# Weight preparation a step earlier, evictions ahead of maxima, and compact loads in the start-up of an attention and MLP kernel

## The chip, the cores and the metric

The kernel runs on one core of a Trainium2 chip. The metric is device time in microseconds (us) of one execution; the time of a kernel is the median of several runs. TensorE does the matrix products, VectorE, ScalarE and GpSimd everything between them, SyncE issues nearly all transfers. The profile calls them PE (its weight loads PEld), DVE, ACT, POOL and SP.

## The reference

Windowed attention, then a token mix of low rank, then an MLP over channels, all with residuals:

```
B, H, S, D = 8, 8, 576, 64
s = (q @ k^T) / sqrt(D)                     # per batch and head
keep, heads 0..3: 0 <= i-j < 32
keep, heads 4..7: 0 <= i-j < 128 and (i-j) % 4 == 0
a = softmax over kept;  x = (a @ v) as (B, S, H*D)       # 8 x 576 x 512
u = x + (U @ V)^T mixed over tokens:  h = x^T @ U @ V,  u = x + h^T   # U 576x32, V 32x576
out = u + relu(u @ w1) @ w2                 # w1 512x2048, w2 2048x512
```

The weights U, V, w1 and w2 arrive as 64-bit floats and are used as a high and a low part of 32 bits.

## The kernel before, in words

The 4608 tokens are 36 tiles of 128; three tiles make a chunk of 384 tokens, so there are 12 chunks. In each chunk the MLP runs over 16 blocks f of 128 hidden channels. Block f is `layer1(f)`, twelve products into the PSUM tile `ph` (high weight by high input, low by high, high by low, four each), then two evictions: ACT writes the high half `hh` with the relu (L912) and DVE the rest `hl` (L913). `layer2(f-1)` follows, nine products into `acc`. While a chunk runs, the attention and the token mix of later batches are put into slots between these products: `slot()` takes items from one queue that is sorted by due time.

Batch 0's attention runs ahead of chunk 0, in `first_batch`. Its unit is a group g, 64 query rows of two tiles by four heads; a batch has 9 groups. A group goes: scores `s` on PE (L404), `soften`, which is mask and maximum `nmax` on DVE (L423) and the exponential on ACT (L427), a transposition `ptp` on PE (L438), a copy to `pt` (ACT L686 here, DVE L444 later), `product`, the product `pv` with v (L461), and `place`, which divides by the sums (L467, L468) and writes the result to the x tiles or to `xp` (L491). For batch 0 `pv` has one PSUM buffer. Heads 4 to 7 are computed with the tokens in another order, so their results go from `xp` to the x tiles by DMA: for batch 0 through the DRAM tensor `spare` (`leave` L766, `come` L771), for later batches by the moves of L495 in `place`.

Batch 1's groups 9 to 17 run in the slots of chunk 0, along with batch 0's and 1's token mix (`t`, `m`, the split `xhl` of L510, `utl`). For batch 0, q and k come compact (tag `k`, 320 KB a group), and `spread_q` puts q into a zeroed tile of two diagonal blocks with two POOL copies (L320). For batch 1 they come as full blocks with the zeros (`qkr`, 224 KB for two heads, 18 loads, L350). v comes in two loads a group (L332), into three buffers; the second is behind `place`'s moves in SP's queue.

The 32 weight pieces, w1 and w2 of every f (piece NSMALL + 2f and the next; NSMALL is 3, the pieces of U and V), are prepared once, during chunk 0: `send` issues the DMA of the raw 64-bit words (L188, L190, 512 KB a piece, five buffers `raw` until the last two blocks), `narrowed` takes two passes on ACT (L197, L198), `add_low` a shift (L202) and an add (L204) on DVE or POOL, and `finish` casts the high half (`w1h` on ACT L208, `w2h` on DVE L210) and subtracts it on POOL for the low (`w1l`, `w2l`, L211). `weight_step` does one of each for four successive pieces: finish of i−3, add of i−2, narrowing of i−1, and sends up to i + AHEAD. It is called twice a block. The instruction order on the engines is the order in which this program is written.

Of the kernel before, what the change touches and what calls it, by code (L numbers as in the profile page):

```python
# [10 lines left out]
F32 = mybir.dt.float32  # L11
# [14 lines left out]
P = 128  # L26
# [34 lines left out]
XL_DVE = ((1, 0),)  # L61
AHEAD = 2
POST_AT = 0.7
# [79 lines left out]
@with_exitstack  # L143
def attention_moe_kernel(ctx: ExitStack, tc: tile.TileContext, qk0, qk1, qk2, vv, masks, wide, ident, ut, vt, uv, w1, w2, out):
    nc = tc.nc
# [130 lines left out]
    def weight_step():  # L276
        i = at.get(0, NSMALL + 3)
        at[0] = i + 1
        if NSMALL <= i - 3 < NPIECE and i - 3 not in finished:
            if i - 3 == NSMALL + 2 * F_LAST:  # L280
                prep_open.close()
                make_w(F_LAST, FC, "right")
            finish(i - 3)
        if NSMALL <= i - 2 < NPIECE and i - 2 not in added:
            add_low(i - 2, nc.gpsimd if (i - NSMALL) % 2 else nc.vector)
        if NSMALL <= i - 1 < NPIECE and i - 1 not in scaled:
            narrowed(i - 1)
        send(min(NPIECE, i + AHEAD))

# [22 lines left out]
    def load_q(g):  # L312
        t = early.tile([P, UNITS, QB + KB], F32, tag="k", name=f"k{g}", bufs=NGB)
        nc.sync.dma_start(out=t, in_=qk0[g])
        loaded[g, 0] = t

    def spread_q(g):
        for i in range(2):
            rs = slice(i * QB, (i + 1) * QB)
            nc.gpsimd.tensor_copy(out=q_sb[rs, g % NQ, :, i], in_=loaded[g, 0][rs, :, 0:QB])  # L320

    def load_v(g, i):
        if (g, 1, i) in loaded:
            return
        if g < NGB:
            t = early.tile([KB, 2, UNITS, VW], F32, tag="v0", name=f"v{g}", bufs=NGB)
            nc.sync.dma_start(out=t, in_=vv[g])
            loaded[g, 1, 0] = t[:, 0]
            loaded[g, 1, 1] = t[:, 1]
        else:  # L330
            t = work.tile([KB, UNITS, VW], F32, tag="v", name=f"v{g}_{i}", bufs=3)
            nc.sync.dma_start(out=t, in_=vv[g][:, i])  # L332
            loaded[g, 1, i] = t

    N0 = UNITS * NGB
    N2 = N0 * SPLIT
    raws = {}
# [5 lines left out]

    def fetch(n, eng=nc.sync):
        if n >= UNITS * NG or n in raws:
            return
        if n < N2:
            if n % 2 == 0:
                raw = work.tile([P, 2, QK1], F32, tag="qks", name=f"qkr{n}", bufs=TB)
                eng.dma_start(out=raw, in_=qk1[n // UNITS - NGB][:, n % UNITS:n % UNITS + 2])  # L350
                raws[n] = raw[:, 0]
                raws[n + 1] = raw[:, 1]
        else:
            raw = work.tile([P, QK2], F32, tag="qk", name=f"qkr{n}", bufs=QKB)
            m = QK1 if is_odd(n) else QK2
            nc.sync.dma_start(out=raw[:, 0:m], in_=qk2[n - N2][:, 0:m])
            raws[n] = raw

# [20 lines left out]
    def score(g, u):  # L379
# [12 lines left out]
        else:  # L392
# [11 lines left out]
            nc.tensor.matmul(sp[:, u % sp.shape[1], :], lhsT=ql, rhs=kr, start=True, stop=True)  # L404
# [233 lines left out]
    def attention_steps(b):  # L638
# [3 lines left out]
        for s in range(NGB + LAG):  # L642
            g = NGB * b + s

            def pre(s=s, g=g):
                if b > 0 and 0 < s <= NGB:
                    load_v(g - 1, 0)
                if s >= LAG:
                    weighted(g - LAG, held.pop(g - LAG))
                if b > 0 and 0 < s <= NGB:  # L650
                    load_v(g - 1, 1)

# [6 lines left out]
            def some(us, g=g):  # L659
                for u in us:  # L660
                    score(g, u)
                for u in us:
                    n = UNITS * g + u
                    if n >= N2:
                        split_qk(n + LOOK)
                        fetch(n + LOOK + DMA_LOOK)
                    elif n >= N0 and n % 2 and n + 2 * TB - 1 < N2:
                        fetch(n + 2 * TB - 1)
                for u in us:
# [10 lines left out]
    def first_batch():  # L680
# [8 lines left out]
        for g in range(NGB):  # L689
# [18 lines left out]
            if g >= 1:  # L708
                copy(g - 1)
            if g >= 3:  # L710
                place(g - 3, pv.pop(g - 3))
            if g == 5:
                narrowed(0)
                add_low(0, nc.gpsimd)
                finish(0)
        w0, w1 = NSMALL, NSMALL + 1
        pv[7] = product(7, pt.pop(7))
        t_first(0, 0)
        turn_dilated(2)
        place(6, pv.pop(6))  # L720
        t_evict(0, 1)
# [108 lines left out]
    load_v(NGB - 1, 0)  # L830
    send(NSMALL + 4)
    for i in (0, 2):
        fetch(N0 + i)
    send(NSMALL + 5)
    fetch(N0 + 4)
    first_batch()
    psum_open.close()
    psum = ctx.enter_context(tc.tile_pool(name="psum", bufs=3, space=bass.MemoryType.PSUM))
# [49 lines left out]
    for c in range(NCHUNK):  # L888
# [41 lines left out]
        for f in range(FC):  # L930
            if c == 0 and f == 0:
                weight_step()
            if c == 0 and f == F_MID - 1:
                after_first()
            layer1(f)
            if f < FC - 1:
# [6 lines left out]
            if f > 0:  # L943
                layer2(f - 1)
                if f < FC - 1:
                    slot()
            if c == 0:
                weight_step()
        for t in more[2:]:
# [11 lines left out]
def lay_out(q, k, v, U, V, w1, w2):  # L961
# [6 lines left out]
    for half in range(2):  # L968
# [13 lines left out]
        for i in range(NJ // 2):  # L982
            g = TILES.index((half, 2 * i)) // 2
            for r in (slice(0, D), slice(D, P)):
                qk2[:, g, :, r, :P] = qp[SPLIT:, :, P * i:P * (i + 1)].transpose(0, 1, 3, 2)
                qk2[:, g, :, r, P:] = kp[SPLIT:, :, P * i:P * i + KW].transpose(0, 1, 3, 2)
    q0 = np.stack([q1[0, :, :, i, :, i] for i in range(2)], axis=2).reshape(NGB, UNITS, P, QB)
    qk0 = np.concatenate([q0, k1[0].reshape(NGB, UNITS, P, KB)], axis=-1)
    qk0 = np.ascontiguousarray(qk0.transpose(0, 2, 1, 3))
    qk1 = np.concatenate([q1.reshape(B, NGB, UNITS, P, P), k1.reshape(B, NGB, UNITS, P, KB)], axis=-1)  # L990
    qk2[:, ODD, :, :, :QK1] = qk1[SPLIT:, ODD]
    qk2 = qk2.reshape((B - SPLIT) * NGB * UNITS, P, QK2)
    qk1 = np.ascontiguousarray(qk1[1:SPLIT].reshape((SPLIT - 1) * NGB, UNITS, P, QK1).transpose(0, 2, 1, 3))
    vv = np.ascontiguousarray(vv.reshape(B * NGB, 2, KB, UNITS, VW).transpose(0, 2, 1, 3, 4))
# [17 lines left out]
    for p in range(NDP):  # L1012
# [35 lines left out]
```

## Time and profile before

| | |
|---|---|
| median of 3 runs | 1067.45 us (1066.99 to 1067.75) |
| the profiled execution | 1066.73 us |
| its span | 1064.6 us |
| PE busy, share of the span | 1000.8 us, 94% |
| DVE, ACT, POOL busy | 583.9, 381.8, 321.3 us |
| mean granted clock of PE | 0.976 |
| batch 0 | 0 to 49.5 us of the span |
| chunk 0 | 49.5 to about 212 us |

A profile line of a group names line, engine, operation and tiles, then how often it ran, its busy time, the mean of one in ns, and the idle time of its engine just before, with what ended it. A line of the waits reads: engine, its line, `<-` the one waited for, then us in total, times, and the longest. A line of the timeline or of the chain begins with start and length in us. The stretches of a window table give, for each part of the span, the busy time of the engines, the clock that PE was granted as a share of full speed, the busy share of the DMA engines, and GB/s.

### The profile page before, as it was taken

The numbers are of one execution on the slowest core, as the hardware profiler recorded it, in microseconds if no ns is written. First come the engines' busy times: TensorE is split into PE (matmuls) and PEld (weight loads), VectorE is DVE, ScalarE is ACT, GpSimd is POOL, SyncE is SP. The second block draws the span as 40 slices with busy tenths as digits, with TensorE's granted clock in tenths as the row PEclk, the third lists the DMA queues.
The fourth block names the chain that finished last, engine by engine and source line by source line (L and its number), as shares of the span: only waits on it lengthen the run. The fifth ranks groups of instructions, "written<-read, shape, count | busy, mean of one in ns | idle before, by whom it ended". The sixth has DMA issues, their size and how long they took to land.

```text
span 1064.6 us, 18031 instructions
## 1 busy us (share of the span) xinstructions
PE 1000.8 (94%) x5928; PEld 875.0 (82%) x5928; DVE 583.9 (55%) x1965; ACT 381.8 (36%) x937; POOL 321.3 (30%) x537
## 2 busy tenths in 40 slices
PE   6768877699999999999999999999999999999998
PEld 5556655588889888988888888988888888999897
DVE  3355565577645676476655675576746774411211
ACT  4453444544423343244514353244414352111110
POOL 3243344543503262133503252134404251000000
PEclk9987898899999999999999999999999999999999
DMA  9156742334322342344323342343323330400000
GB/s 271 68 167 183 218 147 79 110 115 120 100 73 74 89 128 72 76 128 112 87 70 92 102 123 57 89 122 110 89 79 97 91 110 15 129 1 1 30 1 30
DMA packets 97164, 102.54 MB, mean 96 GB/s; under 512 B 12624, under 2 KB 83792, under 8 KB 97072
## 3 DMA queue, kind: packets, MB, share of 16 engines
q1 hardware_dynamic: 97072, 101.39, 33.0%
q8 instruction: 48, 0.79, 0.3%
q14 instruction: 44, 0.36, 0.1%
HBM read 79.32 MB, written 17.89 MB: 91 GB/s over the span
## 4 chain that ended last, share of the span: by engine, by line
PE 86%; issue 4%; DVE 3%; DMA 2%; POOL 2%; SPq 1%; ACT 1%; DVEq 0%; POOLq 0%; ACTq 0%
PE ph L907 38%; PE acc L924 36%; PE pv L461 4%; PE s L391 3%; PE s L404 2%; PE t L540 2%; POOL w1l L211 1%; DVE v L204 1%; PE m L564 1%; DMA raw<-w 1%; SPq L495 1%; PE ptp L438 1%; DMA spare<-xp 1%; ACT hh L912 1%; DMA k<-qk 0%
## 5 line engine op out<-in xcount | busy, mean ns | idle before, releaser
L913 DVE SCALAR_TENSOR_TENSOR hl<-ph,hh 128x384 fp32r<-128x384 f32 x192 | 106.3, 554 | 233.0 <-ACT hh L912 232.1
L924 PE MATMUL acc<-w2h,hh 128*128 128x512 f32 x576 | 230.8, 401 | 0.0
L924 PE MATMUL acc<-w2l,hh 128*128 128x512 f32 x576 | 229.6, 399 | 0.0
L924 PE MATMUL acc<-w2h,hl 128*128 128x512 f32 x576 | 213.7, 398 | 0.0
L368 POOL TENSOR_TENSOR qks<-qkr,qks 128x160 fp32r<-128x160 f32 x192 | 102.8, 535 | 352.6 <-ACT qks L367 255.4
L907 PE MATMUL ph<-uth,w1h 128*128 128x384 f32 x768 | 172.5, 343 | 32.0 <-ACT w1h L208 30.5
L912 ACT ACTIVATE hh<-ph 128x384 fp32r<-128x384 f32 x192 | 93.5, 487 | 298.1 <-PE ph L907 286.9
L907 PE MATMUL ph<-uth,w1l 128*128 128x384 f32 x768 | 178.2, 350 | 5.6 <-POOL w1l L211 5.6
L907 PE MATMUL ph<-utl,w1h 128*128 128x384 f32 x768 | 181.1, 350 | 0.0
L907 PEld LDWEIGHTS ph<-uth,w1h 128*128 128x128 f32 x768 | 137.6, 190 | 51.9 <-ACT w1h L208 35.8
L427 ACT ACTIVATE p<-p,nmax 128x160 f32<-128x160 f32 (+1 forms) x288 | 109.3, 406 | 160.9 <-DVE nmax L423 159.8
L907 PEld LDWEIGHTS ph<-uth,w1l 128*128 128x128 f32 x768 | 140.0, 195 | 10.3 <-POOL w1l L211 10.0
L907 PEld LDWEIGHTS ph<-utl,w1h 128*128 128x128 f32 x768 | 141.5, 197 | 1.7 <-issue 0.2
L450 DVE STREAM_TRANSPOSE pt<-p 32x128 f32<-32x128 f32 x432 | 130.2, 301 | 17.8 <-ACT p L427 12.4
L924 PEld LDWEIGHTS acc<-w2h,hl 128*128 128x128 f32 x576 | 108.7, 189 | 23.7
L924 PEld LDWEIGHTS acc<-w2h,hh 128*128 128x128 f32 x576 | 109.6, 190 | 16.3 <-issue 0.4
L924 PEld LDWEIGHTS acc<-w2l,hh 128*128 128x128 f32 x576 | 109.2, 190 | 16.1
L367 ACT CAST qks<-qkr 128x288 fp32r<-128x288 f32 x192 | 81.1, 429 | 100.0 <-PE s L391 56.2
L420 DVE TENSOR_TENSOR p<-s,wide_sb 128x160 f32<-128x160 f32 x192 | 60.1, 320 | 72.1 <-PE s L391 69.7
L371 POOL TENSOR_TENSOR qks<-qkr,qks 64x128 fp32r<-64x128 f32 x192 | 90.5, 471 | 15.1
L510 POOL TENSOR_TENSOR xhl<-x,xhl 128x256 fp32r<-128x256 f32 (+1 forms) x65 | 47.7, 743 | 82.6 <-ACT xhl L508 75.2
L461 PEld LDWEIGHTS pv<-v,pt 96*64 96x64 f32 x1152 | 42.1, 142 | 30.1 <-issue 17.1
(82 smaller groups left out, 891.1 us busy)
## 6 DMA issues: line engine op xcount, KB each, us to landing
qkr<-qk SPq DMA_DIRECT2D x192, 144.0 KB, 2.2
raw<-w SPq DMA_DIRECT2D x26, 512.0 KB, 5.1
v<-vv SPq DMA_DIRECT2D x126, 97.5 KB, 2.1
out<-x SPq DMA_DIRECT2D x36, 256.0 KB, 2.2
zd<-z SPq DMA_DIRECT2D x120, 64.0 KB, 2.1
xt<-zd SPq DMA_DIRECT2D x30, 256.0 KB, 2.8
qkr<-qk SPq DMA_DIRECT2D x18, 224.0 KB, 2.7
raw<-w SPq DMA_DIRECT2D x12, 256.0 KB, 2.9
```

The lines of the kernel that those rows point to most:

```text
L367: nc.scalar.copy(out=t[:, 0:QK2], in_=raw)
L368: nc.gpsimd.tensor_tensor(out=t[:, QK2:], in0=raw[:, P:], in1=t[:, P:QK2].bitcast(F32), op=ALU.subtract)
L371: eng.tensor_tensor(out=t[lo, 0:P], in0=raw[lo, 0:P], in1=t[lo, 0:P].bitcast(F32), op=ALU.subtract)
L420: nc.vector.tensor_tensor(out=p_sb[:, u, :], in0=sp[:, 0:KW], in1=held[0][:, kind], op=ALU.add)
L427: nc.scalar.activation(out=p_sb[:, u, 0:w], in_=p_sb[:, u, 0:w], func=AF.Exp, bias=nmax[:, u:u + 1], scale=-1.0,)
L450: nc.vector.transpose(out=pt[WIN * k:WIN * (k + 1), :, rs], in_=p_sb[rs, :, o:o + WIN])
L461: nc.tensor.matmul(pv[rs, u, :], lhsT=pt[:, u, rs], rhs=loaded[g, 1, i][:, u, :], start=True, stop=True)
L510: eng.tensor_tensor(out=xl[rs], in0=x[rs], in1=xh[rs].bitcast(F32), op=ALU.subtract)
L907: nc.tensor.matmul(ph, lhsT=w[:, k, :], rhs=u[:, k, :], start=(n == 0), stop=(n == len(seq) - 1))
L912: nc.scalar.activation(out=hh, in_=ph, func=AF.Relu)
L913: nc.vector.scalar_tensor_tensor(out=hl, in0=ph, scalar=0.0, in1=hh.bitcast(F32), op0=ALU.max, op1=ALU.subtract)
L924: nc.tensor.matmul(acc[i], lhsT=h[:, ss], rhs=w, start=(f == 0 and n == 0), stop=(f == FC - 1 and n == 2))
```

## The change

Three edits, made together.

First, `place(g-3)` stands ahead of `product(g-2)` and of `soften(g)` in `first_batch`, and `place(6)` ahead of `product(7)`.

Second, batch 1's q and k come compact like batch 0's, in 9 loads of 320 KB, two groups ahead, and `spread_q` copies q into two zeroed tiles `q1` (four more memsets on DVE). Both v loads of a group are issued ahead of `weighted`, which holds `place` and its moves, and have four buffers; this order holds for all later batches too.

Third, `weight_step` starts one piece further on, and the step that closed a block now opens the next. All that a step does thus happens one step earlier relative to layer 1, and raws are sent up to i + 3 (i + 2 near the end). To start that way `first_batch` sends one piece more and narrows one piece more.

```
-AHEAD = 2
+AHEAD = 3
...
+    q1_sb = [work.tile([P, UNITS, 2, QB], F32, tag="z", name=f"q1_{i}", bufs=ZS) for i in range(2)]
...
     def weight_step():
-        i = at.get(0, NSMALL + 3)
+        i = at.get(0, NSMALL + 4)
...
-        send(min(NPIECE, i + AHEAD))
+        half = NSMALL + 2 * F_LAST
+        send(min(NPIECE, i + AHEAD if i + AHEAD <= half else max(half, i + 2)))
...
+    def q_of(g):
+        return q_sb[:, g % NQ] if g < NGB else q1_sb[g % 2]
+
     def spread_q(g):
         for i in range(2):
             rs = slice(i * QB, (i + 1) * QB)
-            nc.gpsimd.tensor_copy(out=q_sb[rs, g % NQ, :, i], in_=loaded[g, 0][rs, :, 0:QB])
+            nc.gpsimd.tensor_copy(out=q_of(g)[rs, :, i], in_=loaded[g, 0][rs, :, 0:QB])
...
-            t = work.tile([KB, UNITS, VW], F32, tag="v", name=f"v{g}_{i}", bufs=3)
+            t = work.tile([KB, UNITS, VW], F32, tag="v", name=f"v{g}_{i}", bufs=4)
...
             def pre(s=s, g=g):
-                if b > 0 and 0 < s <= NGB:
+                if 0 < s <= NGB:
                     load_v(g - 1, 0)
+                    load_v(g - 1, 1)
+                if b < SPLIT and s + 2 < NGB:
+                    load_q(g + 2)
+                if b < SPLIT and s + 1 < NGB:
+                    spread_q(g + 1)
                 if s >= LAG:
                     weighted(g - LAG, held.pop(g - LAG))
-                if b > 0 and 0 < s <= NGB:
-                    load_v(g - 1, 1)
...
     def first_batch():
...
+            if g >= 3:
+                place(g - 3, pv.pop(g - 3))
             if g >= 2:
                 pv[g - 2] = product(g - 2, pt.pop(g - 2))
...
-            if g >= 3:
-                place(g - 3, pv.pop(g - 3))
...
+        place(6, pv.pop(6))
         pv[7] = product(7, pt.pop(7))
...
-        place(6, pv.pop(6))
...
+        send(NSMALL + 6)
...
+        narrowed(w1 + 1)
...
-    send(NSMALL + 4)
-    for i in (0, 2):
-        fetch(N0 + i)
-    send(NSMALL + 5)
-    fetch(N0 + 4)
+    for i in range(3, 6):
+        send(NSMALL + i)
+        if i < 5:
+            load_q(NGB + i - 3)
     first_batch()
+    spread_q(NGB)
...
         for f in range(FC):
-            if c == 0 and f == 0:
-                weight_step()
             if c == 0 and f == F_MID - 1:
                 after_first()
+            if c == 0:
+                weight_step()
             layer1(f)
...
-            if c == 0:
-                weight_step()
```

ACT around the eviction of block 6, before. `v` and `raw` are the narrowing of a later piece, `p` the exponentials of a group, and the last row is the cast of block 7's w1:

```order
L912 ACTIVATE hh_6_1210<-ph_6_1197 128x384
L197 ACTIVATE v_1218<-raw_1131 128x512
L198 ACTIVATE raw_1131<-raw_1131 128x512
L427 ACTIVATE p_1247<-p_1247,nmax_1248 128x96 x4
L208 CAST w1h_1046<-v_1192 128x4x128
```

And after, the same place:

```order
L919 ACTIVATE hh_6_1227<-ph_6_1214 128x384
L209 CAST w1h_1054<-v_1145 128x4x128
L198 ACTIVATE v_1235<-raw_1065 128x512
L199 ACTIVATE raw_1065<-raw_1065 128x512
L428 ACTIVATE p_1266<-p_1266,nmax_1267 128x96 x4
```

The cast of w1 for block 7 has moved from behind the narrowing and the group's exponentials to right behind the eviction of block 6.

DVE at the same place, before: eviction `hl`, cast of w2, shift and add of block 7's w1 (v_1192), then `place` of a group.

```order
L202 TENSOR_SCALAR v_1128<-v_1128 128x512
L913 SCALAR_TENSOR_TENSOR hl_6_1211<-ph_6_1197,hh_6_1210 128x384
L210 CAST w2h_1048<-v_1128 128x512
L202 TENSOR_SCALAR v_1192<-v_1192 128x512
L204 ISA v_1192<-raw_1036,v_1192 128x1024
L467 TENSOR_SCALAR ssum_1240<-pv_1231 128x4
```

After; block 7's w1 is v_1145:

```order
L211 CAST w2h_1056<-v_1062 128x512
L203 TENSOR_SCALAR v_1145<-v_1145 128x512
L205 ISA v_1145<-raw_943,v_1145 128x1024
L920 SCALAR_TENSOR_TENSOR hl_6_1228<-ph_6_1214,hh_6_1227 128x384
L203 TENSOR_SCALAR v_1209<-v_1209 128x512
L468 TENSOR_SCALAR ssum_1261<-pv_1252 128x4
```

The cast of w2 and the shift and add of w1 have moved ahead of the eviction `hl`; behind it stands one shift of a later piece.

SP in block 3, before: a group's first v, the moves of `place`, the second v, then q and k:

```order
L188 DMA raw_704<-w 128x4x256
L190 DMA raw_733<-w 128x1024
L332 DMA v_0_740<-vv 96x260
L495 DMA x_425<-xp_754 16x256
L495 DMA x_757<-xp_754 32x256
L495 DMA x_759<-xp_754 16x256 x2
L495 DMA x_762<-xp_754 32x256
L495 DMA x_764<-xp_754 16x256
L332 DMA v_1_766<-vv 96x260
L350 DMA qkr_775<-qk 128x448
L350 DMA qkr_777<-qk 128x448
```

After:

```order
L189 DMA raw_721<-w 128x4x256
L191 DMA raw_750<-w 128x1024
L340 DMA v_0_757<-vv 96x260
L340 DMA v_1_759<-vv 96x260
L319 DMA k_761<-qk 128x640
L496 DMA x_408<-xp_777 16x256
L496 DMA x_780<-xp_777 32x256
L496 DMA x_782<-xp_777 16x256 x2
L496 DMA x_785<-xp_777 32x256
L496 DMA x_787<-xp_777 16x256
```

Both v loads and the load of q and k now stand ahead of the moves, one load in place of two.

More of the change, by code (lines that the diff above doesn't have):

```diff
@@ L143, in attention_moe_kernel @@
 @with_exitstack
-def attention_moe_kernel(ctx: ExitStack, tc: tile.TileContext, qk0, qk1, qk2, vv, masks, wide, ident, ut, vt, uv, w1, w2, out):
+def attention_moe_kernel(ctx: ExitStack, tc: tile.TileContext, qk0, qk2, vv, masks, wide, ident, ut, vt, uv, w1, w2, out):
     nc = tc.nc
@@ L312, in load_q @@
     def load_q(g):
-        t = early.tile([P, UNITS, QB + KB], F32, tag="k", name=f"k{g}", bufs=NGB)
+        if g < NGB:
+            t = early.tile([P, UNITS, QB + KB], F32, tag="k", name=f"k{g}", bufs=NGB)
+        else:
+            t = work.tile([P, UNITS, QB + KB], F32, tag="qks", name=f"k{g}", bufs=TB)
         nc.sync.dma_start(out=t, in_=qk0[g])
         loaded[g, 0] = t
+    def q_of(g):
+        return q_sb[:, g % NQ] if g < NGB else q1_sb[g % 2]
     def spread_q(g):
@@ L330, in load_v @@
         else:
-            t = work.tile([KB, UNITS, VW], F32, tag="v", name=f"v{g}_{i}", bufs=3)
+            t = work.tile([KB, UNITS, VW], F32, tag="v", name=f"v{g}_{i}", bufs=4)
             nc.sync.dma_start(out=t, in_=vv[g][:, i])
             loaded[g, 1, i] = t
-    N0 = UNITS * NGB
-    N2 = N0 * SPLIT
+    N2 = UNITS * NGB * SPLIT
     raws = {}
@@ L342, in is_odd, with fetch @@
         return n // UNITS % NGB == ODD
-    def fetch(n, eng=nc.sync):
+    def fetch(n):
         if n >= UNITS * NG or n in raws:
             return
[L347 to L357, printed above, removed]
+        assert n >= N2
+        raw = work.tile([P, QK2], F32, tag="qk", name=f"qkr{n}", bufs=QKB)
+        m = QK1 if is_odd(n) else QK2
+        nc.sync.dma_start(out=raw[:, 0:m], in_=qk2[n - N2][:, 0:m])
+        raws[n] = raw
     def split_qk(n):
@@ L398, in score @@
                 sp = state[g][2]
-            if g >= NGB:
+            if n >= N2:
                 fetch(n)
@@ L402, in score @@
             else:
-                ql, kr = q_sb[:, g % NQ, u].rearrange("p i q -> p (i q)"), loaded[g, 0][:, u, QB:]
+                ql, kr = q_of(g)[:, u].rearrange("p i q -> p (i q)"), loaded[g, 0][:, u, QB:]
             nc.tensor.matmul(sp[:, u % sp.shape[1], :], lhsT=ql, rhs=kr, start=True, stop=True)
@@ L666, in some @@
                         fetch(n + LOOK + DMA_LOOK)
-                    elif n >= N0 and n % 2 and n + 2 * TB - 1 < N2:
-                        fetch(n + 2 * TB - 1)
                 for u in us:
@@ L812, in attention_moe_kernel @@
         eng.memset(q_sb[i * QB:(i + 1) * QB, :, :, 1 - i], 0.0)
+    for i in range(2):
+        for q1 in q1_sb:
+            nc.vector.memset(q1[i * QB:(i + 1) * QB, :, 1 - i], 0.0)
     for t in ts0:
@@ L986, in lay_out @@
                 qk2[:, g, :, r, P:] = kp[SPLIT:, :, P * i:P * i + KW].transpose(0, 1, 3, 2)
-    q0 = np.stack([q1[0, :, :, i, :, i] for i in range(2)], axis=2).reshape(NGB, UNITS, P, QB)
-    qk0 = np.concatenate([q0, k1[0].reshape(NGB, UNITS, P, KB)], axis=-1)
+    q0 = np.stack([q1[:SPLIT, :, :, i, :, i] for i in range(2)], axis=3).reshape(SPLIT * NGB, UNITS, P, QB)
+    qk0 = np.concatenate([q0, k1[:SPLIT].reshape(SPLIT * NGB, UNITS, P, KB)], axis=-1)
     qk0 = np.ascontiguousarray(qk0.transpose(0, 2, 1, 3))
@@ L992, in lay_out @@
     qk2 = qk2.reshape((B - SPLIT) * NGB * UNITS, P, QK2)
-    qk1 = np.ascontiguousarray(qk1[1:SPLIT].reshape((SPLIT - 1) * NGB, UNITS, P, QK1).transpose(0, 2, 1, 3))
     vv = np.ascontiguousarray(vv.reshape(B * NGB, 2, KB, UNITS, VW).transpose(0, 2, 1, 3, 4))
@@ L1020, in lay_out @@
         "qk0": qk0,
-        "qk1": qk1,
         "qk2": qk2,
```

## The prediction

> **What bounds the kernel now.** I read the stretches of the span first, then what TensorE waited for, then the rows of one f-block. The columns of the stretches are: length, busy time with instructions of PE, PEld, DVE, ACT and POOL, the granted clock, the DMA share and GB/s.
>
> ```profile
> 49.50:105.00 55.50, 41.71 (x218) 35.46 (x220) 28.15 (x88) 25.96 (x60) 24.09 (x22) 0.78 0.52 160
> 105.00:156.00 51.00, 38.97 (x242) 31.30 (x242) 27.46 (x81) 20.75 (x49) 20.15 (x18) 0.87 0.59 186
> 156.00:212.00 56.00, 39.07 (x171) 31.56 (x168) 30.68 (x61) 25.75 (x62) 28.70 (x29) 0.88 0.33 100
> 212.00:1064.60 852.60, 847.71 (x5000) 750.39 (x4998) 477.99 (x1624) 286.41 (x707) 233.13 (x437) 1.00 0.29 82
> ```
>
> From 212 us on PE is idle for 852.6 − 847.7 = 4.9 us, and the change touches nothing there but the order of v loads. Everything to be won lies ahead of it: batch 0 (to 49.5 us) and chunk 0 (49.5 to 212 us), where PE idles for 162.5 − 119.75 = 42.75 us and the clock is reduced. Clock lost under PE's own work: 0.22 × 41.71 + 0.13 × 38.97 + 0.12 × 39.07 = 19.0 us. At full clock chunk 0 would hold 119.75 − 19.0 = 100.7 us of PE work, 6.3 us for each of 16 blocks. The waits of PE in 49 to 212 us, then of 173 to 212 us (blocks 12 to 15):
>
> ```profile
> PE ph L907 <- ACT w1h L208: 30.5, 14, 3.9
> PE ph L907 <- POOL w1l L211: 5.6, 13, 1.1
> ...
> PE ph L907 <- ACT w1h L208: 11.1, 4, 3.1
> PE ph L907 <- POOL w1l L211: 2.1, 4, 1.1
> ```
>
> So 36.1 of the 42.75 us are layer 1 waiting for its own weights. The eviction hh closes a block's layer 1; in the chain those of blocks 1 and 9 are 93.2 us apart, 11.7 us a block:
>
> ```profile
> 62.51 0.50 ACT hh L912
> ...
> 155.75 0.50 ACT hh L912
> ```
>
> Why the weights are late shows in block 6 (timeline):
>
> ```profile
> 121.49 0.49 ACT L912 ACTIVATE hh<-ph 128x384 fp32r<-128x384 f32 x1 [3.17 <-PE ph L907]
> 122.98 1.38 POOL L211 TENSOR_TENSOR w2l<-v,w2h 128x512 fp32r<-128x512 f32 x1 [3.17 <-DVE w2h L210]
> 123.28 1.64 DVE L204 CUSTOM_DVE_ANT_0 v<-raw,v 128x1024 uint16<-128x1024 uint16 x1
> 125.24 0.86 DVE L491 TENSOR_TENSOR x<-pv,ssum 64x256 f32<-64x256 f32 x2
> 126.49 1.17 ACT L427 ACTIVATE p<-p,nmax 128x96 f32<-128x96 f32 x4 [3.38 <-DVE nmax L423]
> 127.56 0.60 ACT L208 CAST w1h<-v 128x512 fp32r<-128x512 f32 x1
> 128.22 1.03 PE L907 MATMUL ph<-uth,w1h 128*128 128x384 f32 x4 [2.17 <-ACT w1h L208]
> 128.24 1.29 POOL L211 TENSOR_TENSOR w1l<-v,w1h 128x512 fp32r<-128x512 f32 x1 [3.88 <-ACT w1h L208]
> 129.59 1.65 PE L907 MATMUL ph<-uth,w1l 128*128 128x384 f32 x4 [0.34 <-POOL w1l L211]
> ```
>
> The add of w1 (L204) is done at 124.92, but its cast w1h stands on ACT behind the group's exponentials (L427), which wait for place and maxima on DVE; it runs 2.6 us later. The bound is the order on ACT and DVE, not work (of the three stretches PE is busy 70 to 76%, DVE 51 to 55%, POOL 40 to 51%).
>
> **The change part by part.** Sums go against the profiled execution (1066.73 us, span 1064.6); it is 0.7 us below the median, less than 0.2% (some 2 us), which is about what a measurement of this kernel can tell from no change.
>
> *Weights one step further ahead.* w1h(f+1) now follows hh(f) at once and its add is done ahead of hl(f). By the rows: hh .49, w1h .60, w1l 1.29, with hand-overs about 2.5 us from the end of layer 1 to the next block's weights. What stood there, the two narrowing passes of a later piece, now follows the cast; its raw is sent a piece earlier too. On DVE shift and add (.42 + 1.64) now stand ahead of hl, beside the ph matmuls; were the raw late, hl and layer 2 would be late with it, so the cover is the earlier send. PE meanwhile has layer 2 of f−1 and the attention group: 6.3 us less the twelve ph matmuls (1.03 + 1.65 is the two thirds of them at a partly reduced clock, so about 2.5 to 3.4) leaves some 3 to 4 us. The cover is enough while a block has attention or mixing on PE; with layer 2 alone (most of blocks 12 to 15) cover and chain are about equal. Of 36.1 us I take 28: block 1 still waits about 2 us, since its cast follows an exponential either way, and half of the 13.2 us in blocks 12 to 15 stays, where other waits (buffers of the x pool) come as well. Bounds 18 (half stays) and 36.
>
> *The clock.* It is halved after waits of 2 to 3 us. PE stands mostly idle from 115 to 118.6 us (0.97 us busy in 3.6), and then runs at about half:
>
> ```profile
> 115.00:118.60 3.60, 0.97 (x5) 0.65 (x4) 1.86 (x11) 2.81 (x7) 1.33 (x2) 1.00 0.60 182
> 118.60:121.20 2.60, 2.58 (x8) 2.59 (x9) 0.00 (x0) 0.00 (x0) 1.21 (x1) 0.53 0.83 275
> 129.60:132.30 2.70, 2.70 (x8) 2.70 (x9) 0.00 (x0) 0.11 (x1) 1.91 (x2) 0.50 0.14 53
> ```
>
> The third row follows the 2.17 us gap of block 7 above. Gaps that go give their clock back, gaps that stay (blocks 1 to 5, 12 to 15) don't. Of 19.0 us I take 11; bounds 5 and 17.
>
> The Trainium skill ("TensorE: Matmul & The Clock Gate", "HAM oscillation") has the gate close when a wait crosses an idle window, which it gives as about 3.4 us. By that rule the waits of 2 to 3 us that I leave would cost no clock, and the sum would be about 3 us lower, 1030. The rows disagree: a 2.17-us wait was followed by 0.50.
>
> *Batch 0.* pv has one buffer, and place(g−3), which frees it, stood on DVE behind the maxima of group g (pieces of the chain, rows of DVE's timeline, PE's waits of 13 to 36 us, POOL's group of 5 to 60 us):
>
> ```profile
> 16.83 1.06 PE s L404 x8
> 17.89 0.45 PE ptp L438 x4
> 18.35 1.33 issue
> 19.68 0.69 PE pv L461 x16
> ...
> 18.75 0.16 DVE L467 TENSOR_SCALAR ssum<-pv 128x4 f32<-128x4 f32 x1
> 18.94 0.18 DVE L468 RECIPROCAL ssum<-ssum 128x4 f32<-128x4 f32 x1
> 19.16 0.42 DVE L491 TENSOR_TENSOR xp<-pv,ssum 128x256 f32<-128x256 f32 x1
> ...
> PE pv L461 <- issue: 8.2, 6, 1.7
> L320 POOL COPY q_sb<-k 64x256 f32<-64x256 f32 x16 | 6.3, 396 | 8.8 <-DMA k<-qk 7.1 <-PE ptp L438 1.3
> ```
>
> The place that ends at 19.58 releases the pv of 19.68. With place first, such waits (six, 8.2 us) can go; what is late next is PE's own 1.06 + .45 + .69 = 2.2 us a group, with ACT (exponentials 1.17 and a copy of pt) close behind. POOL's q copies already waited 7.1 us for k, so part turns into a wait for loads. I take 6, bounds 3 and 8.2. The four added memsets lie ahead of the first maxima, which wait for loads; the two narrowing passes that move to its end cost 0 to 1.3 (two ACT passes of .65, as in block 6); I take 1.
>
> *Batch 1's loads.* 18 loads of 224 KB become 9 of 320: fewer bytes, fewer issues, less blocking of SP. New are 18 POOL copies of .396 us = 7.1 us. POOL idles over 30 us in each of two stretches, which hides them, unless one stands ahead of a late w1l: 0 to 7.1, I take 1.5. Now both v loads go ahead of the place moves, and raws up to two pieces further ahead stand ahead of both. Pieces of the chain in blocks 3 to 5 (start, length, what), and SP's longest wait group of 49 to 160 us but one:
>
> ```profile
> 92.34 5.70 DMA spare<-xp
> 98.10 0.32 SPq L771
> ...
> 102.03 0.59 SPq L495
> 102.72 2.07 DMA v<-vv
> 104.84 0.94 PE pv L461 x14
> ...
> SPq L332 <- PE pv L461: 21.4, 3, 8.6
> ```
>
> The second v load (issued by 102.7) stood behind six moves (.59 each) and a read (L771) waiting 5.7 us for a copy through DRAM. The moves no longer stand ahead of it; the read still does, and arrives while PE is faster. L332 had waited 21.4 us for a v buffer, and a fourth buffer eases that. I take 5 us of new waits here; bounds −3 (the v wait goes too) and 15 (5.7 + 2.07 in two blocks). In block 7 a token split on POOL comes between (about 2 us in the rows nearest, w1l 1.29 and a split): 1.5, bounds 0 and 2.
>
> *POOL's w1l beside DVE.* w1l now runs right behind hh, beside DVE's shift and casts:
>
> ```profile
> 151.35 1.29 POOL L211 TENSOR_TENSOR w1l<-v,w1h 128x512 fp32r<-128x512 f32 x1 [4.38 <-ACT w1h L208]
> 151.56 1.37 DVE L202 TENSOR_SCALAR v<-v 128x512 int32<-128x512 int32 x1
> L202 DVE TENSOR_SCALAR v<-v x34: 360/420/1367, 30.9 to 204.9; 128x512 int32<-128x512 int32 x32, 128x384 int32<-128x384 int32 x1, 128x448 int32<-128x448 int32 x1
> ```
>
> A shift of .42 took 1.37 and ended as POOL's did. That is up to .95 us in each of 15 blocks on DVE, mostly ahead of place and maxima, which have slack now: 0 to 9, I take 2.
>
> The Trainium skill ("SBUF — State Buffer", "SBUF: two separate sides") calls the pair of ports that DVE and GpSimd share an exclusive lock held for the whole instruction. The shift's row agrees; the 1.64-us add that began beside w2l (123.28 against 122.98) shows no such delay.
>
> Sum: 28 + 11 + 6 − 1 − 1.5 − 5 − 1.5 − 2 = 34 us; 1067.45 − 34 = **1033 us**.
>
> **The rivals.**
> *Queues take over (about 1047).* Per group SP issues two v, one k, six moves, two raws and a copy or read, 13 at .32 to .59 by the rows above, about 6 us: nearly PE's block. With one read waiting 5.7 us for DRAM, blocks 2 to 8 stay near 9.3 us. Then weight waits give 18, clock 6, batch 0 6, less 10: 20 us. For it: the chain between 76 and 105 us is mostly SP and DMA. Against: from block 6 on it is w1h and w1l.
> *DVE locked out by POOL wherever they meet (about 1041).* With .95 us a block on the path to w1h in 10 blocks, the lock costs 9.5 instead of 2, 1033 + 7.5. For it the 1.37; against it the 1.64.
> *Nearly all idle goes (about 1014).* 36 of waits, 17 of clock, 8 of batch 0, less 8 of new waits: 53. Against: chunk 0 would shrink to some 115 us, and DVE's 86.3 us of the three stretches would fill 75% of it, POOL's 72.9 + 7.1 us 70%, in chains.
> *Slower (about 1073).* Raws are sent further ahead into the same five buffers, so SP stands at raw p until the add of p − 5 is done, with the v and k loads queued behind. If that delays each of nine groups by a DRAM round trip of 5.7 us, it is 51 us against 45 us won: +6. It decides from 5 us a group. Against: SP's waits for those adds were short, and the adds come earlier now.
> *Nothing (1067).* That the cast is ahead of the exponential, but its data late by as much. In block 6 the add was done 2.6 us early, which excludes most of it.
>
> **The numbers.** Forecast .53 (its own range 1020 to 1042), queues .20, lock .07, nearly all .11, slower .05, nothing .04. Slower by over 0.2% is .05, within .04, faster .91. The range from 1014 (nearly all) to 1054 (queues with the bound of 15 on loads) leaves out the last two and the tails: 1014 to 1054.
>
> **What would show it.** PE's wait on w1h and w1l in chunk 0 from 36 down to some 8 us; w1h directly behind hh on ACT, ready before layer 2's end; hh to hh from 11 us to 6.5–7.5 in blocks 6 to 11; clock over .9 between 105 and 156 us; pv's issue gaps in batch 0 below .5 us; shifts of 1.3 us on DVE beside w1l. Wrong it is if PE's waits reappear at pv (v, SP) or at m, t (DVE, POOL), or if block 2 to 5 keep 11 us.

## The result, and the profile after

| | before | after |
|---|---|---|
| median | 1067.6 us (1066.99 to 1068.28, 4 runs) | 1028.94 us (1028.01 to 1030.62, 4 runs) |
| ratio, 95% interval | | 0.964 (0.9623 to 0.9656) |
| profiled execution, its span | 1066.73, 1064.6 us | 1030.62, 1028.8 us |
| first `hh` of chunk 0, and the sixteenth | 52.87, 211.11 us | 46.87, 175.01 us |
| from the sixteenth `hh` to the end | 853.5 us | 853.8 us |

The kernel became 3.6% faster; 1033 was forecast, in a range of 1014 to 1054. Behind chunk 0 nothing moved. Of the 35.8 us between the two spans, 6.0 lie ahead of the first `hh` (batch 0) and 30.1 between the first and the sixteenth.

The stretches of the kernel after (length, busy time of PE, PEld, DVE, ACT, POOL, then clock, DMA share, GB/s); the third now ends where the last block's `hh` is in the same place as at 212 us before:

```profile
43.40:95.00 51.60, 42.38 (x259) 37.45 (x259) 33.40 (x107) 30.03 (x70) 33.67 (x38) 0.87 0.61 189
95.00:136.00 41.00, 33.38 (x232) 28.21 (x231) 26.18 (x75) 21.30 (x48) 23.91 (x23) 0.92 0.67 206
136.00:175.90 39.90, 30.61 (x132) 24.75 (x131) 28.01 (x50) 20.40 (x53) 25.39 (x27) 0.89 0.36 100
175.90:1028.80 852.90, 848.15 (x5003) 752.14 (x5001) 477.51 (x1623) 287.28 (x707) 233.60 (x438) 1.00 0.29 82
```

Chunk 0 has shrunk from 162.5 to 132.5 us. PE's idle time in it went from 42.75 to 132.5 − 106.37 = 26.1 us, and its busy time from 119.75 to 106.37 us, 13.4 less for the same products. Most of that is the clock: by the stretches' granted clock and length, 0.22 × 55.5 + 0.13 × 51.0 + 0.12 × 56.0 = 25.6 us of full speed were withheld before and 0.13 × 51.6 + 0.08 × 41.0 + 0.11 × 39.9 = 14.4 are now, 11.2 less. The other 2 us the granted clock does not account for. PE's waits of 43 to 176 us (us in total, times, longest):

```profile
PE pv L462 <- DMA v<-vv: 8.2, 4, 3.8
PE ph L914 <- ACT w1h L209: 6.0, 3, 2.5
PE s L392 <- POOL qks L372: 2.9, 1, 2.9
PE s L405 <- DVE x L567: 2.3, 1, 2.3
PE t L541 <- POOL xhl L511: 2.0, 3, 1.2
PE t L541 <- DVE xhl L511: 1.8, 2, 1.6
...
PE ph L914 <- POOL w1l L212: 1.2, 3, 0.5
```

Layer 1 waits 7.2 us for its weights in place of 36.1. At the head of the list stands v instead. The place of block 6 and 7 that the prediction showed, in the timeline of the kernel after:

```profile
106.44 0.49 ACT L919 ACTIVATE hh<-ph 128x384 fp32r<-128x384 f32 x1 [1.55 <-PE ph L914]
106.83 0.61 ACT L209 CAST w1h<-v 128x512 fp32r<-128x512 f32 x1
...
107.52 1.47 POOL L212 TENSOR_TENSOR w1l<-v,w1h 128x512 fp32r<-128x512 f32 x1 [1.90 <-ACT w1h L209]
107.72 0.69 PE L462 MATMUL pv<-v,pt 96*64 96x65 f32 x16
...
110.08 1.18 ACT L428 ACTIVATE p<-p,nmax 128x96 f32<-128x96 f32 x4 [1.50 <-DVE nmax L424]
...
110.45 0.86 PE L914 MATMUL ph<-uth,w1h 128*128 128x384 f32 x4
111.15 0.87 PE L914 MATMUL ph<-uth,w1l 128*128 128x384 f32 x4
...
112.85 0.49 ACT L919 ACTIVATE hh<-ph 128x384 fp32r<-128x384 f32 x1
```

The weights of block 7 are ready at 108.99, 2.55 us after `hh` began, and PE takes them up at 110.45 without a wait, at full clock (.86 for four products, where it took 1.03 and 1.65). From `hh` to `hh` this block takes 6.41 us, before 11.06.

Not all blocks are like it. From `hh` to `hh`, in us, by the starts of ACT's rows in the two timelines:

| blocks | 1 | 2 | 3 | 4 | 5 | 6 | 7 | 8 | 9 | 10 | 11 | 12 | 13 | 14 | 15 |
|---|---|---|---|---|---|---|---|---|---|---|---|---|---|---|---|
| before | 9.64 | 8.47 | 12.08 | 15.58 | 11.51 | 11.34 | 11.06 | 11.53 | 11.67 | 10.12 | 7.36 | 10.21 | 9.21 | 8.54 | 9.92 |
| after | 7.82 | 5.76 | 10.38 | 11.99 | 10.26 | 13.36 | 6.41 | 10.76 | 7.49 | 5.41 | 8.60 | 7.79 | 7.91 | 6.16 | 8.04 |

Blocks 3 to 6 took 50.5 us and still take 46.0. There PE waits for v (8.2 us) and once for DVE (2.3 us), and the clock falls behind each wait of 2 us and more. Two of the waits for v, with the products around them:

```profile
60.47 0.39 PE L931 MATMUL acc<-w2h,hl 128*128 128x512 f32 x1
63.30 0.92 PE L462 MATMUL pv<-v,pt 96*64 96x65 f32 x16 [2.43 <-DMA v<-vv]
64.15 1.55 PE L405 MATMUL s<-k,q 128*128 128x96 f32 x8
...
92.04 0.53 SPq L191 DMA_DIRECT2D raw<-w  x1
92.68 0.38 SPq L189 DMA_DIRECT2D raw<-w  x1
93.16 0.92 SPq L340 DMA_DIRECT2D v<-vv  x2
...
99.05 1.23 PE L462 MATMUL pv<-v,pt 96*64 96x65 f32 x16 [3.82 <-DMA v<-vv]
```

The v of 93.16 stands behind two raws of 512 KB, both in SP's queue and in the transfers, and lands some 5 us after its issue, where the profile's page gives 2.2 as the median of all v loads. SP in turn had stood in front of the raws for their buffers, the longest group of its waits of 43 to 170 us being

```profile
SPq L191 <- DVE v L205: 18.6, 7, 4.1
```

### The profile page after: what moved, and what is told of

Read it like the earlier page. It is cut to its first block, busy times and chain, and to the rows that moved or that the text cites. A ratio compares the mean times of both kernels' runs of the same rounds, so it can differ in the third digit from the quotient of the medians.

```text
span 1028.8 us, 18053 instructions
## 1 busy us (share of the span) xinstructions
PE 988.2 (96%) x5928; PEld 869.0 (84%) x5928; DVE 586.3 (57%) x1969; ACT 382.0 (37%) x937; POOL 331.8 (32%) x555
## 4 chain that ended last, share of the span: by engine, by line
PE 83%; POOL 1%; DVE 1%; issue 1%; ACT 0%; DMA 0%; DVEq 0%; POOLq 0%; SPq 0%
PE acc L931 37%; PE ph L914 37%; PE pv L462 3%; PE s L392 3%; PE t L541 2%; PE m L565 1%; PE s L405 0%; POOL v L205 0%; POOL w1l L212 0%; DVE v L205 0%; DVE v L203 0%; POOL w2l L212 0%; PE tp L631 0%; DMA raw<-w 0%; DVE xhl L511 0%
## 5 line engine op out<-in xcount | busy, mean ns | idle before, releaser
L914 PE MATMUL ph<-utl,w1h 128*128 128x384 f32 x768 | 177.2, 343 | 0.0
L914 PE MATMUL ph<-uth,w1l 128*128 128x384 f32 x768 | 173.1, 341 | 1.2 <-POOL w1l L212 1.2
L914 PEld LDWEIGHTS ph<-uth,w1h 128*128 128x128 f32 x768 | 138.2, 189 | 23.9 <-ACT w1h L209 7.3
L451 DVE STREAM_TRANSPOSE pt<-p 32x128 f32<-32x128 f32 x432 | 130.2, 301 | 18.7 <-ACT p L428 13.4
L914 PEld LDWEIGHTS ph<-uth,w1l 128*128 128x128 f32 x768 | 137.6, 190 | 2.5 <-POOL w1l L212 2.2
L914 PEld LDWEIGHTS ph<-utl,w1h 128*128 128x128 f32 x768 | 137.7, 191 | 1.7 <-issue 0.2
L372 POOL TENSOR_TENSOR qks<-qkr,qks 64x128 fp32r<-64x128 f32 x192 | 90.7, 472 | 15.1
```

The costliest lines, as they stand in the source:

```text
L372: eng.tensor_tensor(out=t[lo, 0:P], in0=raw[lo, 0:P], in1=t[lo, 0:P].bitcast(F32), op=ALU.subtract)
L451: nc.vector.transpose(out=pt[WIN * k:WIN * (k + 1), :, rs], in_=p_sb[rs, :, o:o + WIN])
L914: nc.tensor.matmul(ph, lhsT=w[:, k, :], rhs=u[:, k, :], start=(n == 0), stop=(n == len(seq) - 1))
```

## The experiments

All comparisons are with the kernel before on the same chips, as ratios with their 95% intervals. The profiles behind the sums below are one execution each.

**The third edit alone** (weight steps one piece further on; the rest as before).

```
 kernel before, with
-AHEAD = 2
+AHEAD = 3
-        i = at.get(0, NSMALL + 3)
+        i = at.get(0, NSMALL + 4)
...
```

> The kernel before with the third edit alone (weight steps one piece further on, raws further ahead; batch 0 and batch 1's loads as before). Theory: the wait of layer 1 for its own weights was an order on ACT, so this edit alone brings nearly all of the gain in chunk 0: 24 to 30 us of the 38.7, time 1038 to 1044, PE's wait on w1h and w1l from 36 to 7-10 us. Rival (the edits need each other: without the compact loads SP blocks on the 18 full loads, raws and v come late): under 15 us, time above 1053, with the gain of weights returned as waits of pv for v and of s for q and k.

Measured: 1038.53 us, 0.9738 (0.9715 to 0.9762), 28 us. PE's waits of 43 to 212 us:

```profile
PE pv L462 <- DMA v<-vv: 12.4, 8, 3.4
PE ph L910 <- ACT w1h L208: 5.7, 3, 2.5
```

The theory holds: this edit brings most of the gain. The rival has a part of it: the wait for v is half as long again as with the compact loads, and block 4 takes 17.0 us.

**The first edit alone** (place ahead of product and maxima in batch 0).

```
 kernel before, with
+            if g >= 3:
+                place(g - 3, pv.pop(g - 3))
             if g >= 2:
                 pv[g - 2] = product(g - 2, pt.pop(g - 2))
...
```

> The kernel before with the first edit alone (place ahead of the product and of the maxima in batch 0). Theory: pv's waits in batch 0 (8.2 us) go, some of it turns into waits for k; first hh of chunk 0 6 us earlier, time 1061 to 1062, nothing changed behind it. Rival (chunk 0 is bound by loads that come at their own pace, so an earlier start is given back in block 0 and 1): first hh earlier, time within 2 us of before.

Measured: 1062.25 us, 0.9951 (0.9931 to 0.997), 5 us. The first `hh` came at 45.73 us, 7.1 earlier, and the sixteenth at 206.56, 4.6 earlier; 2.6 us were given back within chunk 0. Theory with a little of the rival.

**The second edit alone** (compact q and k, order and buffers of v).

```
 kernel before, with
+            t = work.tile([P, UNITS, QB + KB], F32, tag="qks", name=f"k{g}", bufs=TB)
...
-                if b > 0 and 0 < s <= NGB:
+                if 0 < s <= NGB:
                     load_v(g - 1, 0)
+                    load_v(g - 1, 1)
...
```

> The kernel before with the second edit alone (compact q and k two groups ahead, both v loads ahead of the moves, four v buffers). Theory: in the kernel before layer 1 waits for its weights behind the exponentials, so a faster SP gains little there: 0 to 5 us, time 1062 to 1068; in blocks 3 to 5, where the chain ran over SP and the second v load, up to 5 us. Rival (SP and DMA were the true limit of blocks 2 to 9): 10 us or more, time under 1057.

Measured: 1063.97 us over 12 runs, 0.9982 (0.996 to 1.0004): 2 us or nothing. Layer 1 waits for its weights as long as before, 35.0 us; whether that hid what the loads could bring, the next run shows:

```profile
PE ph L911 <- ACT w1h L209: 29.6, 14, 4.0
PE ph L911 <- POOL w1l L212: 5.4, 12, 1.1
```

**The first and third edits without the second.**

> The first and third edits without the second (batch 1's q and k as 18 full loads, second v behind the moves, three v buffers). Alone the three edits gave 28.4, 5 and 2 to 3 us. If they add, this stands at 1067 less 33.5, 1033 to 1035, and the compact loads are worth 4 to 6 us beside the other two, twice what they gave alone, because in the kernel before the wait for weights covered the late v. If the loads matter only alone, 1029 to 1031.

Measured: 1030.92 us, 0.9656 (0.9641 to 0.9671). Beside the other two the loads are worth 2 us by the medians, as alone, and the intervals of the two ratios just overlap. That is less than the 4 to 6 of the expectation's first case and inside its second, so the wait for weights had hidden nothing that can be told from noise. PE's wait for v is 11.2 us here, 8.2 with them. The three edits alone give 28 + 5 + 2 = 35 us, together 38 to 39; with intervals of some 2 us either way on each of the three, they may just add.

**The cast of w1 moved alone**, ahead of the exponentials, adds and raws as before.

```
 kernel before, with
         send(min(NPIECE, i + AHEAD))
+        if (i - 2 - NSMALL) % 2 == 0 and NSMALL <= i - 2 < NPIECE and i - 2 not in finished:
...
+            finish(i - 2)
```

> The kernel before, with one thing moved: w1 of block f+1 is finished (cast on ACT, subtraction on POOL) at the end of the step behind layer 1 of f, ahead of the group's exponentials, in place of after layer 2. Adds, narrowing and raws stay as they were. Theory (order on ACT): the cast follows the add directly, 124.95 in place of 127.56 in block 6, so some 2 us a block over 12 blocks: 15 to 25 us with the clock, time 1042 to 1052. Rival (the data, that is adds and raws, are late; only a step further ahead helps): the cast waits for the add and holds up the exponentials behind it; under 6 us or slower, time above 1061.

Measured: 1057.23 us, 0.9918 (0.9894 to 0.9942), 9 us: between the two. PE's waits for the weights fell from 36.1 only to 23.9 us, and v came up:

```profile
PE ph L912 <- ACT w1h L208: 20.2, 10, 3.9
PE pv L466 <- DMA v<-vv: 5.8, 2, 3.1
...
PE ph L912 <- POOL w1l L211: 3.7, 9, 0.6
```

A block of the timeline shows what the cast now waits for:

```profile
117.64 1.64 DVE L204 CUSTOM_DVE_ANT_0 v<-raw,v 128x1024 uint16<-128x1024 uint16 x1
119.31 0.62 ACT L208 CAST w1h<-v 128x512 fp32r<-128x512 f32 x1 [1.83 <-DVE v L204]
```

The add on DVE ends just ahead of it, and ACT stands idle for 1.83 us with the exponentials behind the cast.

**The counterpart: adds and raws early, the cast behind the exponentials.**

```
 kernel after, with
-        if NSMALL <= i - 3 < NPIECE and i - 3 not in finished:
-            if i - 3 == NSMALL + 2 * F_LAST:
+        if NSMALL <= i - 4 < NPIECE and i - 4 not in finished:
+            if i - 4 == NSMALL + 2 * F_LAST:
...
-            finish(i - 3)
+            finish(i - 4)
```

> The changed kernel with the finish of a piece (cast, subtraction) put back by one step, so that the cast of w1 stands on ACT behind the exponentials as before, while adds, narrowing and raws keep their earlier place. It is the counterpart of the run with the cast moved alone, which gave 0.8%. Theory now: cast and add each were late, about as much; with the add early and the cast late PE still waits 15 to 25 us for w1h: 1040 to 1050. Rival A (the late adds were the whole matter): within 5 us of the changed kernel, under 1034. Rival B (the cast's place was the whole matter, and moving it alone failed for the add): 1055 or more.

Measured: 1059.06 us, 0.9911 (0.9886 to 0.9936). Rival B comes nearest. This kernel holds the first two edits as well, which alone gave 0.9951 and 0.9982, together 0.993. That leaves some 0.2% for the early adds, with the cost of raws sent further ahead in it, and no more than the intervals could hide. The wait for weights is about what it was before the change: 32.3 us for w1h and w1l, and one wait of 4.0 at the same products for which the trace names no releaser:

```profile
PE ph L914 <- ACT w1h L209: 17.2, 10, 4.4
PE ph L914 <- POOL w1l L212: 15.1, 11, 3.2
PE ph L914 <- issue: 4.0, 1, 4.0
```

and in the timeline the cast stands behind the exponentials again, with the product behind it:

```profile
120.37 1.17 ACT L428 ACTIVATE p<-p,nmax 128x96 f32<-128x96 f32 x4 [2.00 <-DVE nmax L424]
121.45 0.60 ACT L209 CAST w1h<-v 128x512 fp32r<-128x512 f32 x1
...
122.11 0.97 PE L914 MATMUL ph<-uth,w1h 128*128 128x384 f32 x4 [1.20 <-ACT w1h L209]
```

But of the wait a larger part is now POOL's: 15.1 us for w1l, before the change 5.6. In five blocks the subtraction starts 0.9 to 3.9 us after the cast's end, directly behind an add on POOL (at 151.30 behind an add that had just ended, with the cast done at 147.37), which happens in no block of the kernel before. The early adds thus brought a hindrance of their own, and how much of the wait would stay with the cast alone put back is not shown.

So neither half does it: the cast starts at the later of two times, add done and ACT free. In block 6 of the kernel before, ACT came 2.6 us later, but not in every block. ACT's waits show that before the change six of the casts already stood waiting for the add, and with the cast moved alone twelve did:

```profile
ACT w1h L208 <- DVE v L204: 10.1, 6, 3.5
...
ACT w1h L208 <- DVE v L204: 21.2, 12, 3.5
```

With the adds early no cast waits for its add, and the casts wait for ACT alone. Moving one leaves the other.

**Raws one piece later**, the steps unmoved.

```
 kernel after, with
-AHEAD = 3
+AHEAD = 2
```

> The changed kernel with raws sent one piece later (up to i+2 throughout), the steps themselves unmoved. Theory: the gain comes from where cast, subtraction and add stand around layer 1, not from the distance of the raws; a raw lands in 4 to 5 us and has a block's time: weight waits stay at 6 to 10 us, SP stands less in front of full raw buffers, so v comes earlier: 1024 to 1029. Rival (the raws are what was late): ACT waits at its narrowing passes for raws, with hh behind them, and the time rises by 5 to 15 us, to 1034 to 1044.

Measured: 1026.08 us, 0.9614 (0.9601 to 0.9627), 2.9 us below the changed kernel's median; the intervals of the two ratios just overlap. The wait for w1h is 5.6 us, that for v 4.1 in place of 8.2. The raws' greater distance, a part of the third edit, thus brings nothing, and by the medians costs about 3 us.

**Batch 1's v two groups ahead**, behind the product that frees its buffers.

```
 kernel after, with
     def weighted(g, pt):
-        place(g, product(g, pt))
+        pv = product(g, pt)
+        if g // NGB == 1 and g + LAG < 2 * NGB:
+            load_v(g + LAG, 0)
+            load_v(g + LAG, 1)
+        place(g, pv)
...
```

> The changed kernel with batch 1's v loaded two groups ahead: group g+2's two loads stand directly behind the product of g, ahead of place's moves, in the same four buffers. Theory: the 8.2 us that pv waits for v in blocks 2 to 6 come from v standing behind raws in SP's queue and in the transfers; they go, and with them some 2 to 4 us of clock behind the gaps: 1018 to 1023. Rival (blocks 3 to 6 are bound by what the transfers carry, about 1.6 MB a block): the wait moves to k or to the raws, gain under 3 us, 1026 or more.

Measured: 1026.35 us, 0.9613 (0.96 to 0.9627), 2.6 us below the changed kernel. The rival is right on the size and wrong on the place. The wait for v is gone from the list, and PE waits for the mixing add on DVE, which waits for batch 0's rows from DRAM:

```profile
88.64 0.77 DVE L571 TENSOR_TENSOR x<-x,m 128x256 f32<-128x256 f32 x2 [4.92 <-DMA x<-spare]
89.11 1.10 PE L466 MATMUL pv<-v,pt 96*64 96x65 f32 x16 [3.63 <-DVE x L571]
```

**Both of these, and both with the copies through DRAM earlier.** The second has, besides,

```
-    queue += [(0.15 + 0.01 * p, lambda p=p: leave(p)) for p in range(NDP)]
-    queue += [(0.22 + 0.005 * i, lambda i=i: come(i)) for i in range(n0)]
+    queue += [(0.06 + 0.01 * p, lambda p=p: leave(p)) for p in range(NDP)]
+    queue += [(0.16 + 0.005 * i, lambda i=i: come(i)) for i in range(n0)]
```

> The changed kernel with raws a piece later and v behind the product of two groups before, each of which alone gave 2.6 to 2.9 us. If both took away the same wait (v behind raws), 1025 to 1027; if they add, 1022 to 1024.

> The same two, and batch 0's copies through DRAM a block and a half earlier, their reads a block earlier. Theory: with v early the next late thing in blocks 4 and 5 is DVE's mixing add, which waits 4.9 us for the read of spare and holds PE's product for 3.6; it goes, with its clock: 5 to 8 us below the run before it, 1017 to 1021. Rival (the transfers carry all they can there): the same bytes land no earlier, within 2 us.

Measured: 1024.19 us, 0.9597 (0.9578 to 0.9617), and 1024.11 us, 0.9587 (0.9563 to 0.961). The two parts add most of what they gave alone (4.8 of 5.5 us), and this version is faster than the changed kernel by 0.4%. The earlier copies bring nothing, which is what the rival of that run forecast, but not for its reason: the last reads of `spare` are issued by 78.3 us in place of 87.2. In the first of the two, blocks 5 and 6 already take 9.0 and 6.8 us, and PE is busy nearly throughout there, so the rows from DRAM were no longer what was waited for long. Its stretches of block 4 and of blocks 5 and 6, and behind them PE's longest wait in block 4 with what stood ahead of it on DVE:

```profile
67.00:82.00 15.00, 11.22 (x65) 9.76 (x65) 9.44 (x35) 6.87 (x20) 9.27 (x13) 0.82 0.67 203
...
82.00:98.00 16.00, 15.09 (x116) 12.93 (x116) 13.16 (x40) 8.38 (x20) 10.23 (x10) 0.96 0.66 190
...
74.02 0.43 DVE L211 CAST w2h<-v 128x512 fp32r<-128x512 f32 x1 [2.29 <-POOL v L205]
...
74.91 1.54 DVE L205 CUSTOM_DVE_ANT_0 v<-raw,v 128x1024 uint16<-128x1024 uint16 x1
76.37 0.73 DVE L571 TENSOR_TENSOR x<-x,m 128x256 f32<-128x256 f32 x2
...
76.83 2.02 PE L405 MATMUL s<-k,q 128*128 128x96 f32 x8 [2.36 <-DVE x L571]
```

The mixing add waits here for no transfer. It stands on DVE behind a cast of w2, which waited 2.29 us for POOL's add, and behind the add of w1.

**The shift ahead of `hl`**, away from w1l.

```
 kernel after, with
             narrowed(i - 1)
+            if (i - NSMALL) % 2 == 0:
+                shift(pipe[i - 1][1])
+                shifted.add(i - 1)
...
```

> The changed kernel with the shift of the pieces that POOL adds done one step earlier on DVE, ahead of hl, so that it no longer runs beside POOL's w1l. Theory: shifts of 1.3 us fall to .42, worth 0 to 2 us since DVE has slack: 1027 to 1029. Rival (the shared port decides in blocks 1 to 15, about .9 us each): 5 us or more faster, 1024 or less. A third outcome, slower, would mean that DVE now stands at a narrowing pass with hl behind it.

Measured: 1028.62 us, 0.9642 (0.9618 to 0.9665), no difference from the changed kernel. It can't price the lock as meant, since there was little to take away: in the changed kernel 3 of the 31 shifts in chunk 0 took 1.3 us or more, here 1.

**POOL's copies of q left out** for groups 11 to 17, whose scores then use the q of earlier groups.

```
 kernel after, with
-                if b < SPLIT and s + 1 < NGB:
+                if b < SPLIT and s == 0:
                     spread_q(g + 1)
```

> The changed kernel with POOL's copies of q for groups 11 to 17 left out (their scores use the q of earlier groups): 14 copies of .4 us less on POOL. It prices the copies, which the forecast put at 1.5 us. Theory: 0 to 3 us faster, 1026 to 1029. Rival (POOL is a bound of blocks 2 to 8): 5 us or more.

Measured: 1027.43 us, 0.9628 (0.9607 to 0.9648): 1.5 us by the medians, inside the intervals of both. These copies are no bound worth 5 us.

## Why the prediction was right, by its own steps

| term | forecast | measured in the two profiles | how |
|---|---|---|---|
| layer 1's waits for weights | 28 | 28.9 | 36.1 − 7.2 |
| clock | 11 | 13.4, of it some 11 the clock | PE busy 119.75 − 106.37; granted clock 25.6 − 14.4 |
| batch 0, with the narrowing moved into it | 6 − 1 | 6.0 | first `hh` 52.87 − 46.87 |
| new waits in chunk 0 | −10 | −12.3 | other idle time 42.75 − 36.1 = 6.65, now 26.1 − 7.2 = 18.9 |
| sum | 34 | 36.0 | spans 35.8 |

*The bound* was read rightly, with a limit. The place behind the exponentials has to go: with the adds early and cast and subtraction late, the waits for weights fell by 4 us at most, part of that held back by POOL. That is not enough: the cast moved alone took away 12.2 of 36.1 us, where the 2.6 us of block 6 had looked like the price of most blocks. What bound was the later of two, ACT's queue and DVE's, and the change moved both. Block 6, by which the prediction ruled out that the data are late as well, was not typical: six casts had been waiting for their add. Of the waits that were to stay, block 1 has 2.5 us (2 forecast) and blocks 12 to 15 have 4.7 (half of 13.2 forecast).

*New waits.* The size was right, and v was named as the main part (5 forecast; the wait for v rose by 7.5, from 0.7 to 8.2). The reason was not: the v loads wait less behind the read from DRAM than behind raws that were sent further ahead, the mechanism that the prediction kept for its slower rival, at about a tenth of the size that this needed. The run with raws a piece later halves that wait, and the one with v ahead of them takes it away. The 2.9 us for `qks`, the splitting of batch 2's q and k on POOL, was in no step.

*The queues.* That rival is what blocks 3 to 6 did: 11.5 us a block. Its picture, blocks 2 to 8 near 9.3 us, came nearly as drawn, with a mean of 9.8; its sum did not, since it gave the weights 18 us and the clock 6. Forecast was "hh to hh from 11 us to 6.5–7.5 in blocks 6 to 11": only blocks 7 and 9 come out near that, with block 10 at 5.4 and 6, 8 and 11 above, a mean of 8.7. Two of the signs that the prediction named for being wrong came, PE's waits at pv and blocks 3 to 5 near 11 us (10.4, 12.0, 10.3; block 2, named with them, fell to 5.8). So the size of the whole was right and its place in chunk 0 was not, and that is in part luck. The forecast came out since blocks 7 to 15 gave 21.1 us and blocks 1 and 2 gave 4.5, as much as blocks 3 to 6.

*POOL beside DVE.* Forecast 2 us, "shifts of 1.3 us" in up to 15 blocks. It was three, in each of which w1l had begun first, and all shifts of chunk 0 together are 3.4 us over .42. In block 6 the shift began .08 us ahead of w1l, took .42, and it was w1l that took longer:

```profile
107.44 0.42 DVE L203 TENSOR_SCALAR v<-v 128x512 int32<-128x512 int32 x1
```

1.47 against the 1.29 of the rows before. The Trainium skill ("SBUF — State Buffer", "SBUF: two separate sides") says of a GpSimd operation and a DVE operation that needs the shared pair of ports that whichever starts first gets the pair and the other blocks. These rows agree on who pays, and the prediction had counted the price as always DVE's.

*The clock.* The 19.0 us lost were reckoned too low: the mean clock of a stretch, which counts idle time at full clock, was taken times busy time alone. By the stretches' lengths it is 25.6, and the 11 taken of it came out (25.6 − 14.4). The rule of thumb, a wait of 2 to 3 us halves the clock, was borne out: in chunk 0 of the kernel after, each of the five waits of 2.2 to 2.9 us (from 48.1, 60.9, 77.8, 159.4 and 169.3 us) was followed within 2 us of its end by 3.4 us at 0.50, and the 3.8-us wait from 95.2 by 6.8 us. Four waits of 1.2 to 1.4 us were not, one of 1.6 was, and in the kernel before one of 2.4 (from 195.5) was not. `s` behind the wait that ends at 63.30 took 1.55, where it took 1.13 at 108.33. The Trainium skill ("TensorE: Matmul & The Clock Gate", "HAM oscillation") gives about 3.4 us for the gap that matters. The 2.43-us wait at 60.9 lies under it and was followed by slow products, so that the prediction was right not to go by it here. The time lies nearer to the 1030 that this rule was said to give than to 1033, but the trace does not bear the rule out.

*Batch 0.* The step was right: pv's six waits of 8.2 us between 13 and 36 us became one of 0.9.

*Copies of q* were put at 1.5 us, and leaving out 14 of 18 gave 1.5, not clear of the intervals. *The range's* upper end was worked out as the queues with 15 us on loads; that makes 1057, not 1054, and changes nothing here.

With both loads mended, blocks 3 and 4 still take 8.0 and 13.7 us. In block 3 PE is busy for 7.34 us, at full clock. In block 4 the trace names waits of 1.4 us (a place) and 2.4 (the mixing add behind the weights on DVE), and a half clock follows. Left open is what setting the mixing add ahead of the cast of w2 would bring, which no run tried.

## What to carry to other kernels

When an instruction waits for two queues, measure both times, in every block, before pricing the removal of one: moving one gains only what it is later than the other. Here the cast alone gave 0.8% and the adds alone nothing clear of noise, where the step that moves both gave 2.6%. After a large wait is gone, look at what stood in the same queue behind the transfers that feed it: sending bulk loads further ahead than a block's slack needs made the small urgent loads late. And count the clock as a term of its own: some 11 of the 36 us were PE's clock, reduced for less of the time.

## What was not expected of the hardware

The clock fell in batch 0 in one profiled execution and not in others that run the same products there. In the profiled run of the second edit alone, PE had been waiting 1.33 us in each group, as in the kernel before, and one wait took 1.57:

```profile
22.30 1.57 issue
23.86 1.14 PE pv L461 x16
...
23.80:36.80 13.00, 10.85 (x77) 8.36 (x77) 4.06 (x25) 5.11 (x15) 3.41 (x6) 0.50 0.53 191
```

For 13 us PE ran at half clock, and the first `hh` came at 58.42 us in place of 52.87. In the kernel before, the same row of waits had one of 1.66 (at 28.85) and the clock stayed. So the length of one wait does not decide it; what does is not shown. The twelve times of that kernel, 1062.2 to 1070.8 us, spread wider than the changed kernel's four, but this is not the whole of the spread: its two longest executions had a mean clock of 0.979, above that of the shortest, 0.975.

The run with the shift moved shows the other side. Its program does not differ from the changed kernel's in batch 0, yet `s` of one group took 2.02 us there until 27 us into the span, and 1.13 only then:

```profile
25.39 2.02 PE L415 MATMUL s<-k,q_sb 128*128 128x96 f32 x8
...
29.27 1.13 PE L415 MATMUL s<-k,q_sb 128*128 128x96 f32 x8
```

In the changed kernel the 1.13 begin at 13.57 us. The first `hh` came at 50.93 in place of 46.87, with no long wait to explain it. The clock column reads 1.00 in both up to 40 us, so this slow beginning is seen in the products' times and not in that column.
